# Block attention: reciprocals laid side by side before they are sent, and the tail transpose in a PSUM tile of its own

## The chip, the cores and the metric

The kernel runs on one core of one Trainium2 chip. The metric is device time in microseconds (us), the median of several executions of the whole program; lower is better. One further execution was recorded by the hardware profiler, and every row below comes from it.

## The reference

Three stages in float32. First, attention with a block-causal mask, for 4 batches × 8 heads, 576 positions, 64 features a head; block i of 64 queries sees the keys of blocks 0 to i:

```
scores = q @ k.T / 8;  masked where key block > query block
attn = exp(scores - rowmax) ;  attn /= rowsum + 1e-9
x = attn @ v                       # 2304 tokens x 512 features
```

Then a dense layer pair, `max(0.01 h, h) @ w_out` with `h = x @ w_in` (512 to 2048 and back), and then a mixture of 8 experts (`relu(x @ w1[e]) @ w2[e]`, 512 to 1024 and back) whose weights P come from a softmax of `x @ w_gate`, normalised eight times by rows and columns.

## The kernel before

**Pairs and turns.** Attention works on two heads at once, a pair; there are 16 pairs (`NP`). A loop over p, from -1 to 16, runs one *turn* for each: in turn p the scores of pair p+1 are made (`scores`), the exponentials of pair p are turned by TensorE so that keys lie on partitions (`turn_attn`, seven groups g = 0 to 6), the last products of pair p-1 with v are made (`weigh`), pair p-1 is divided by its softmax sums and split into two parts (`split_x`, L414 to L425), and q and k of pair p+2 are turned (`turn_q`, `turn_k`, `turn_tail`). The order of these steps on TensorE is the list `turns`, written out by hand; TensorE runs exactly in that order. The order on the other engines and on the DMA queues is laid down when the program is built, by a scheduler with its own estimates. Each engine then takes its instructions in that order, and an instruction that waits holds all that stands behind it.

**Blocks, even and odd.** Of the nine blocks of 64 queries the even ones ("straight") keep head 0 on partitions 0 to 63 and head 1 on 64 to 127, and the odd ones ("crossed") the other way round. `ssum` holds the sums of exponentials, one column a block, and a tenth column that block 8 uses for the second half of its keys.

**The way of the sums.** At the start of turn p, `totals(p)` adds 1e-9 on GpSimd (L357), takes reciprocals on VectorE (L358) into `rsum`, 128 partitions × 9 columns, and sends them to DRAM in two transfers (L362): the five even columns to `row0`, the four odd ones to `row1`. `spread_totals(p)`, late in the turn, reads these rows back four times (L371), each broadcast over 64 partitions, into `by_feature`; VectorE uses that in turn p+1 (L414). All of these transfers are issued by the SP queue. On that queue each turn has, in this order as it ran: the two row transfers, four loads of v (L246, L250), the four reads of the rows, six loads of q and k and their tails (L262, L266), now and then one of a weight (L136, L141), and the next turn's row transfers. There is one q, one k and one tails buffer (`qraw`, `kraw`, `tails`).

**PSUM.** TensorE writes into PSUM tiles: four `sc` tiles for scores, two tiles under the tag "tr", taken in turn, for everything that is transposed (pool `ps_tr`), and one `av` tile of two banks for the products with v. A "tr" tile is free again when whatever was transposed into it has been copied out: groups with even g by ScalarE (L390), with odd g by VectorE (L392), q by ScalarE (L278), k by VectorE (L283).

**The tail.** 576 is four times 128 and 64 more. The last 64 rows of q and k of a pair lie in `tails` and are turned together (L309). From pair 2 on the result goes into the first 128 columns of the `av` tile of pair p-2, which at that point of the order is the current pair's and not written yet; ScalarE copies the q half out (L278) and VectorE the k half (L283). Right behind it in `turns` stands `first_product` (L402, L405), which writes other columns of that same `av` tile.

**Weights.** Beside the turns the float64 words of eight weight pieces are changed into float32 pairs, one small step behind each `scores` (L136 to L202). The dense layers and the experts follow on TensorE.

Of the kernel before, what the change touches and what calls it, by code (L numbers as in the profile page):

```python
# [8 lines left out]
F32 = mybir.dt.float32  # L9
# [6 lines left out]
P = 128  # L16
# [20 lines left out]
def block_attention_mlp_moe(  # L37
# [15 lines left out]
    nc = tc.nc  # L53
# [4 lines left out]
    NQ = S // BLK  # L58
# [156 lines left out]
    def attention(att, ps_sc, ps_tr, ps_av):  # L215
# [13 lines left out]
        ex = [att.tile([P, ew], F32, name=f"ex{i}") for i in range(2)]  # L229
        nmax = [att.tile([P, NQ + 1], F32, name=f"nmax{i}") for i in range(2)]  # L230
        ssum = [att.tile([P, NQ + 1], F32, name=f"ssum{i}") for i in range(2)]
        rsum = [att.tile([P, NQ], F32, name=f"rsum{i}") for i in range(2)]
        NPAR = ((NQ + 1) // 2, NQ // 2)
        by_feature = [[att.tile([P, BLK * n], F32, name=f"by_feature{i}{n}") for n in NPAR] for i in range(2)]
        xs = att.tile([P, S], F32, name="xs")
# [40 lines left out]
        def spread(p, src, lo, n):  # L276
            scale = 1.0 / float(D) ** 0.5
            nc.scalar.activation(  # L278
                out=qT[p % 2][:, lo * BLK:(lo + n) * BLK], in_=src[:, 0:n * BLK], func=AF.Copy, scale=scale
            )  # L280

        def place_k(p, src, lo, hi):
            nc.vector.tensor_copy(out=kT[p % 2][:, lo:hi], in_=src)  # L283
# [3 lines left out]
        def av_tile(p):  # L287
            if p not in av:
                av[p] = ps_av.tile([P, 1024], F32, name="av", tag="av")
            return av[p]  # L290
# [11 lines left out]
            place_k(p, km[:, 0:W], 0, W)  # L302

        def turn_tail(p):
            if 0 <= p - 2:
                tail = av_tile(p - 2)
            else:
                tail = ps_tr.tile([P, 512], F32, name="qk_tail", tag="tr")
            nc.tensor.transpose(tail[:, 0:2 * TAIL], tails, ident)  # L309
            spread(p, tail, W // BLK, TAIL // BLK)  # L310
            place_k(p, tail[:, TAIL:2 * TAIL], W, S)
# [41 lines left out]
        rows = {}  # L353

        def totals(p):
            r, s = rsum[p % 2], ssum[p % 2][:, 0:NQ]
            nc.gpsimd.tensor_scalar(out=r, in0=s, scalar1=EPS, scalar2=None, op0=ALU.add)  # L357
            nc.vector.reciprocal(out=r, in_=r)  # L358
            rows[p] = []
            for c, n in enumerate(NPAR):  # L360
                t = dram.tile([2, BLK * n], F32, name=f"row{c}", tag=f"row{c}")
                nc.sync.dma_start(out=t.rearrange("h (q i) -> (h q) i", i=n), in_=r[:, c:NQ:2])  # L362
                rows[p].append(t)

        def spread_totals(p):
# [67 lines left out]
        def first_product(p):  # L433
# [5 lines left out]
            ("nxt", scores, 3, 2), *other_parts[2:], ("prv", split_x), ("nxt", load_v), ("cur", turn_attn, 1),  # L439
            ("nxt", scores, 5, 4), ("cur", turn_attn, 2), ("fol", turn_q),  # L440
            ("nxt", scores, 1, 0), ("fol", turn_tail), ("cur", first_product), ("cur", turn_attn, 3),
            ("nxt", scores, 7, 6), ("fol", turn_k), ("cur", turn_attn, 4),
            ("cur", spread_totals), ("cur", turn_attn, 5), ("cur", turn_attn, 6),
        ]
        opening = [
            ("nxt", scores, 1, 0), ("nxt", scores, 3, 2), ("nxt", scores, 5, 4), ("nxt", scores, 8),
            ("fol", turn_q), ("nxt", scores, 7, 6), ("nxt", load_v), ("fol", turn_k), ("fol", turn_tail),
        ]

# [13 lines left out]
        turn_q(0)  # L463
        turn_k(0)
        turn_tail(0)
        warm(ps_sc, "sc", 3)
        load_qk(1)
# [3 lines left out]
        for p in range(-1, NP + 1):  # L471
            who = {"prv": p - 1, "cur": p, "nxt": p + 1, "fol": p + 2}
            if 0 <= p < NP:
                totals(p)
            if p == NP:
                first_product(p - 1)
            for w, f, *a in (turns if p >= 0 else opening):
                if 0 <= who[w] < NP and (f is not first_product or p < NP - 1):
                    f(who[w], *a)
                if f is scores and p >= 0 and steps:  # L480
                    with ExitStack() as queued:
                        if p + 1 < NP:
                            queued.enter_context(tc.issue_after(getattr(latest[0], "ins", latest[0])))
                        steps.pop(0)()
            if p + 3 < NP:
                load_qk(p + 3)
# [50 lines left out]
    with (  # L537
        tc.tile_pool(name="att", bufs=1) as att,
        tc.tile_pool(name="ps_sc", bufs=4, space=bass.MemoryType.PSUM) as ps_sc,
        tc.tile_pool(name="ps_tr", bufs=2, space=bass.MemoryType.PSUM) as ps_tr,  # L540
        tc.tile_pool(name="ps_av", bufs=1, space=bass.MemoryType.PSUM) as ps_av,
    ):
        with tc.manual_schedule(engines={mybir.EngineType.PE}):
            attention(att, ps_sc, ps_tr, ps_av)
# [677 lines left out]
    for n in range(0, NGR, 2):  # L1222
        p, e, i = groups[n]
# [135 lines left out]
```

## Time and profile before

| | |
|---|---|
| median of 3 runs | 2149.96 us (2146.71 to 2151.47) |
| the profiled execution | 2146.18 us |
| its span, first to last instruction | 2144.4 us |
| TensorE busy, share of the span | 2073.6 us, 97% |
| VectorE, ScalarE, GpSimd busy | 1561.2, 816.5, 654.3 us |
| mean granted TensorE clock | 0.983 of full speed |

The page cuts the span into 40 slices of 53.6 us. In the first six, attention, TensorE is busy 7 or 8 tenths and its clock stands between 0.7 and 0.9 of full speed; from the seventh on it is busy 9 tenths or more at full clock. So the shares of the whole span say little about attention, which has to be read by itself. A turn is measured below from the first score product of block 8 (64x288) to the next one.

### The profile page before, as it was taken

How to read it: one execution, taken by the hardware profiler on the slowest of the kernel's cores; microseconds unless marked ns; L12 is line 12 of the kernel's file. 1: busy time of each engine (PE TensorE's matmuls, PEld its weight loads, DVE VectorE, ACT ScalarE, POOL GpSimd, SP SyncE). 2: the span in 40 equal slices, each digit the busy share in tenths (PEclk: the TensorE clock that was granted, in tenths of full speed). 3: DMA queues.
4: the chain of work that ended last, by engine and by line, in shares of the span. 5: the costliest groups of instructions: out<-in, count | busy, mean ns of one | idle time of the engine just before them, and what ended most of it. 6: DMA issues, size and time to landing. Idle time of an engine off the chain costs nothing.

```text
span 2144.4 us, 32404 instructions
## 1 busy us (share of the span) xinstructions
PE 2073.6 (97%) x11498; PEld 1853.6 (86%) x11498; DVE 1561.2 (73%) x2687; ACT 816.5 (38%) x1795; POOL 654.3 (31%) x639
## 2 busy tenths in 40 slices
PE   8777799999999999999999999999999999999999
PEld 4333368898879888998999999999999999999998
DVE  6554547565644888777878688888888688888886
ACT  5444433222233544544554433223333433333222
POOL 1111213122201354445444133332332223333322
PEclk9897899999999999999999999999999999999999
DMA  5454422011103788888889777777777677777773
GB/s 114 77 86 72 76 43 60 30 60 30 50 10 123 275 320 297 297 307 316 297 297 342 283 276 256 268 254 254 257 270 279 241 259 252 266 263 257 267 257 111
DMA packets 254945, 436.92 MB, mean 204 GB/s; under 512 B 95016, under 2 KB 135976, under 8 KB 254528
## 3 DMA queue, kind: packets, MB, share of 16 engines
q1 hardware_dynamic: 253584, 434.56, 60.8%
q8 instruction: 91, 1.49, 0.3%
q14 instruction: 70, 0.57, 0.1%
q10 hardware_dynamic: 1200, 0.30, 0.1%
HBM read 308.82 MB, written 125.95 MB: 203 GB/s over the span
## 4 chain that ended last, share of the span: by engine, by line
PE 87%; DMA 5%; DVE 4%; ACT 1%; issue 1%; SPq 1%; POOL 0%; DVEq 0%; ACTq 0%; POOLq 0%
PE h_ps L854 28%; PE o L1022 20%; PE o L1078 12%; PE o L533 9%; PE h_ps L513 9%; PE o L854 3%; DMA row<-rsum 2%; PE sc L331 2%; DMA kraw<-in_k_dram 1%; PE tr L383 1%; PE av L405 1%; DMA by_feature<-row 1%; DVE nmax L337 1%; DMA wraw<-in_moe_w_out_dram 1%; DVE xa L951 0%
## 5 line engine op out<-in xcount | busy, mean ns | idle before, releaser
L951 DVE TENSOR_TENSOR xa<-o,xa 128x384 f32<-128x384 f32 x392 | 216.0, 552 | 110.5 <-PE o L1022 106.7
L854 PE MATMUL h_ps<-xhS,w1h 128*128 128x384 f32 x768 | 257.5, 335 | 0.0
L854 PE MATMUL h_ps<-xhS,w1l 128*128 128x384 f32 x768 | 256.6, 334 | 0.0
L854 PE MATMUL h_ps<-xlS,w1h 128*128 128x384 f32 x768 | 256.6, 334 | 0.0
L951 POOL TENSOR_TENSOR xa<-xa 128x384 f32<-128x384 f32 x92 | 106.0, 1152 | 408.1 <-DVE xa L951 370.8
L951 ACT COPY places<-h_ps 128x384 f32<-128x384 f32 x192 | 92.3, 481 | 287.0 <-PE h_ps L854 219.6
L951 ACT CAST xllate<-xa 128x384 fp32r<-128x384 f32 x120 | 61.6, 514 | 279.2 <-POOL xa L951 279.2
L854 PE MATMUL h_ps<-xhA,w1h 128*128 128x384 f32 x448 | 150.8, 337 | 0.1
L854 PE MATMUL h_ps<-xhA,w1l 128*128 128x384 f32 x448 | 150.0, 335 | 0.0
L854 PE MATMUL h_ps<-xlA,w1h 128*128 128x384 f32 x448 | 149.9, 335 | 0.0
L854 PEld LDWEIGHTS h_ps<-xhS,w1h 128*128 128x128 f32 x768 | 144.2, 188 | 0.7 <-issue 0.6
L854 PEld LDWEIGHTS h_ps<-xlS,w1h 128*128 128x128 f32 x768 | 144.2, 188 | 0.0
L854 PEld LDWEIGHTS h_ps<-xhS,w1l 128*128 128x128 f32 x768 | 144.1, 188 | 0.0
L1078 PE MATMUL o<-w2h,xhlate 128*128 128x512 f32 x408 | 143.8, 391 | 0.0
L951 POOL TENSOR_TENSOR places<-places 128x384 f32<-128x384 f32 x60 | 60.9, 1014 | 251.0 <-DVE wa L951 234.0
L1078 PE MATMUL o<-w2h,xllate 128*128 128x512 f32 x384 | 133.9, 389 | 0.0
L1022 PE MATMUL o<-xllate,w2h 128*128 128x384 f32 x480 | 122.4, 335 | 0.0
L1022 PE MATMUL o<-xhlate,w2h 128*128 128x384 f32 x480 | 121.8, 334 | 0.0
L768 POOL TENSOR_TENSOR wa<-wraw 128x256 f32<-128x256 f32 x32 | 29.8, 931 | 296.4 <-DVE w1l L786 279.1
L533 PE MATMUL o<-hh,w2h 128*128 128x512 f32 (+1 forms) x320 | 117.8, 369 | 0.0
L533 PE MATMUL o<-hh,w2l 128*128 128x512 f32 (+1 forms) x320 | 117.7, 368 | 0.0
L521 DVE TENSOR_TENSOR g<-h_ps,g 128x512 f32<-128x512 f32 (+1 forms) x80 | 50.9, 636 | 90.4 <-ACT g L520 90.1
(261 smaller groups left out, 5731.1 us busy)
## 6 DMA issues: line engine op xcount, KB each, us to landing
wraw<-in_moe_w_dram SPq DMA_DIRECT2D x64, 512.0 KB, 4.6
w1h<-k_1h SPq DMA_DIRECT2D x64, 512.0 KB, 5.3
w1l<-k_1l SPq DMA_DIRECT2D x64, 512.0 KB, 6.1
w2h<-k_1h SPq DMA_DIRECT2D x60, 512.0 KB, 6.1
w2l<-k_1l SPq DMA_DIRECT2D x60, 512.0 KB, 6.8
w1h<-k_0h SPq DMA_DIRECT2D x64, 384.0 KB, 3.8
w1l<-k_0l SPq DMA_DIRECT2D x64, 384.0 KB, 4.1
w2h<-k_0h SPq DMA_DIRECT2D x60, 384.0 KB, 4.3
```

Source lines behind the costliest of these rows:

```text
L331: nc.tensor.matmul(sc[o:o + BLK, :], qT[p % 2][r, i * BLK:(i + 1) * BLK], kT[p % 2][r, lo:hi], start=True, stop=True,)
L337: latest[0] = nc.vector.tensor_reduce(out=nm[:, i + s:i + s + 1], in_=sc, axis=AX.X, op=ALU.max, negate=True)
L383: nc.tensor.transpose(tr[:, s].rearrange("p h q -> p (h q)"), ex[p % 2][:, off[i] + c * P:off[i] + (c + 1) * P], swap if i in crossed else ...
L405: nc.tensor.matmul(av[p][r, 512 + P * max(c - 1, 0):512 + S - P], lhsT, a[:, q0:, :], start=c == 0, stop=c == NKC - 1,)
L513: nc.tensor.matmul(ps[:, 0:n], w[:, c, cols], x, start=c == 0 and s == 0, stop=c == KC - 1 and s == 2,)
L521: nc.vector.tensor_tensor(out=g[:, 0:n], in0=ps[:, 0:n], in1=g[:, 0:n], op=ALU.max)
L533: nc.tensor.matmul(ps[:, 0:n], w[:, cut], h[:, 0:n], start=start and m == 0, stop=stop and m == 2)
L768: nc.gpsimd.tensor_tensor(out=one[:, 0], in0=a21, in1=a22, op=ALU.add)
L854: mm = nc.tensor.matmul(ps, w[:, c], x[:, c], start=first and c == 0 and s == 0, stop=c == 1 and s == 2, skip_group_check=True,)
L951: ins = f(*a, **k)
L1022: mm = nc.tensor.matmul(o, a, b, start=i == 0, stop=i == 5)
L1078: mm = nc.tensor.matmul(o, h, w, start=m == 0, stop=m == 11)
```

## The change

Two things. `rsum` becomes 128 × 2 × 5: the sums are read as (even columns, odd columns), so that the five straight reciprocals of a partition lie next to each other and the crossed ones behind them; all ten columns are added to and inverted instead of nine. Each of the two row transfers then reads neighbouring elements of a partition. And `turn_tail` always takes a tile of `ps_tr` (tag "tr") instead of borrowing the `av` tile.

```
-        rsum = [att.tile([P, NQ], F32, name=f"rsum{i}") for i in range(2)]
+        rsum = [att.tile([P, 2, (NQ + 1) // 2], F32, name=f"rsum{i}") for i in range(2)]
...
         def turn_tail(p):
-            if 0 <= p - 2:
-                tail = av_tile(p - 2)
-            else:
-                tail = ps_tr.tile([P, 512], F32, name="qk_tail", tag="tr")
+            tail = ps_tr.tile([P, 512], F32, name="qk_tail", tag="tr")
             nc.tensor.transpose(tail[:, 0:2 * TAIL], tails, ident)
...
         def totals(p):
-            r, s = rsum[p % 2], ssum[p % 2][:, 0:NQ]
+            r, s = rsum[p % 2], ssum[p % 2].rearrange("p (i c) -> p c i", c=2)
             nc.gpsimd.tensor_scalar(out=r, in0=s, scalar1=EPS, scalar2=None, op0=ALU.add)
             nc.vector.reciprocal(out=r, in_=r)
...
-                nc.sync.dma_start(out=t.rearrange("h (q i) -> (h q) i", i=n), in_=r[:, c:NQ:2])
+                nc.sync.dma_start(out=t.rearrange("h (q i) -> (h q) i", i=n), in_=r[:, c, 0:n])
```

## Rows read from the trace of the kernel before

**Rows 1.** Stretches: start:end, length, busy time of each engine, clock, DMA share.

```profile
core 0: us, PE busy (x) PEld busy (x) DVE busy (x) ACT busy (x) POOL busy (x), PEclk, DMA share, GB/s
13.64:26.41 12.77, 10.37 (x82) 5.60 (x82) 7.69 (x20) 7.48 (x27) 0.73 (x3) 1.00 0.36 72
26.41:268.49 242.08, 184.58 (x1275) 91.88 (x1274) 133.26 (x292) 112.00 (x363) 46.05 (x59) 0.86 0.48 80
44.95:62.00 17.05, 13.73 (x99) 6.71 (x98) 10.63 (x24) 8.77 (x28) 1.84 (x3) 0.90 0.54 98
99.22:115.77 16.55, 13.69 (x100) 6.90 (x99) 9.26 (x22) 8.36 (x27) 3.40 (x6) 0.90 0.90 74
209.91:226.41 16.50, 13.18 (x100) 6.65 (x99) 10.12 (x24) 8.87 (x29) 2.16 (x4) 0.93 0.44 96
187.55:209.91 22.36, 15.90 (x100) 8.13 (x99) 10.18 (x23) 8.87 (x29) 5.09 (x6) 0.75 0.37 60
310.00:2144.40 1834.40, 1828.55 (x9823) 1721.43 (x9821) 1391.01 (x2309) 673.48 (x1341) 600.68 (x552) 1.00 0.64 225
```

**Rows 2.** TensorE's waits from 13 to 270 us: total us, times, longest.

```profile
PE av L402 <- DVE kT L283: 25.0, 14, 2.6
PE qm L295 <- DVE at L392: 14.6, 8, 3.3
PE tr L383 <- DVE kT L283: 13.1, 12, 1.5
PE km L301 <- DMA kraw<-in_k_dram: 6.4, 4, 2.6
```

**Rows 3.** VectorE's waits from 26.41 to 268.49 us, same columns.

```profile
DVE xs L414 <- DMA by_feature<-row: 12.1, 8, 3.5
```

**Rows 4.** Waits of the SP queue from 13 to 300 us, same columns.

```profile
SPq L371 <- DMA row<-rsum: 114.6, 21, 8.1
```

**Rows 5.** Timeline of the SP queue, one round: start, length, what is issued.

```profile
86.79 1.26 SPq L362 DMA_DIRECT2D row<-rsum  x2
...
90.05 0.50 SPq L250 DMA_DIRECT2D vraw<-in_v_dram  x1
96.73 2.91 SPq L371 DMA_DIRECT2D by_feature<-row  x4
...
104.44 0.56 SPq L362 DMA_DIRECT2D row<-rsum  x1
```

**Rows 6.** Transfers of the whole kernel: KB each, median us from issue to landing.

```profile
DMA packets 254945, 436.92 MB, mean 204 GB/s; under 512 B 95016, under 2 KB 135976, under 8 KB 254528
...
out_dram<-xa SPq DMA_DIRECT2D x18, 256.0 KB, 2.0
...
kraw<-in_k_dram SPq DMA_DIRECT2D x30, 128.0 KB, 2.9
...
row<-rsum SPq DMA_DIRECT2D x16, 2.5 KB, 10.8
row<-rsum SPq DMA_DIRECT2D x16, 2.0 KB, 11.8
```

**Rows 7.** The instructions that touch rsum, and its transfers' landing times.

```profile
L357 POOL TENSOR_SCALAR rsum<-ssum x16: 242/242/296, 14.1 to 282.8; 128x9 f32<-128x9 f32 x16
...
DMA to landing us min/median/max: 8.9/11.1/12.6
```

**Rows 8.** Timeline around the tail of one turn, all engines.

```profile
106.60 0.33 PE L309 MATMUL av<-ident,tails 128*128 128x128 f32 x1
106.67 0.58 ACT L390 COPY at<-tr 128x512 f32<-128x512 f32 x1
...
107.64 0.60 ACT L278 ACTIVATE qT<-qm 128x512 f32<-128x512 f32 x1
...
108.39 0.23 DVE L283 COPY kT<-av 128x64 f32<-128x64 f32 x1 [1.25 <-ACT qT L278]
...
108.67 0.44 PE L402 MATMUL av<-at,vraw 128*64 128x128 f32 x4 [1.74 <-DVE kT L283]
```

**Rows 9.** Timeline of TensorE in the first turn.

```profile
20.68 0.44 PE L402 MATMUL av<-at,vraw 128*64 128x128 f32 x4 [0.91 <-DVE kT L283]
```

## The prediction

> **What bounds the kernel now.** I read the stretches first. From 310 us on TensorE is busy 1828.6 of 1834.4 us at full clock [rows 1]: nothing in the change touches that part, so whatever attention gives back should come off the end one for one. Attention is another matter. Between the first turn and 268.49 us there are 13 turns in 242.08 us, 18.62 us each, with TensorE busy 76% of the time at a mean clock of 0.86 [rows 1]. Six of these turns are short, 16.46 to 17.05 us, mean 16.70 (the first and last of the six are shown, and one between them); the other seven reach from 18.48 to 22.36 us, and the longest stands in the rows [rows 1]. Short and long mostly alternate, which points to something with a fixed period beside TensorE.
>
> The waits say what it is. TensorE's own list names two kinds [rows 2]. One comes in every turn: the first product with v waits for VectorE's copy of the k tail, 25.0 us in 14 waits. The other comes in the long turns: q's transpose waits for VectorE (14.6 us, 8 times) and k's for its load (6.4 us, 4 times). VectorE was late there because it had itself stood waiting for the rows read back from DRAM, 12.1 us in 8 waits [rows 3]. And these were late because the SP queue stood still: its reads of the rows wait for the rows to land, 114.6 us in all, up to 8.1 us at a time [rows 4].
>
> One round of that queue shows the period. The row transfers are issued at 86.79, the loads of v behind them until 90.55; then the queue holds until 96.73, reads the rows back, issues q and k, and sends the next rows at 104.44 [rows 5]. That is 17.65 us: 9.94 from the rows to their reading, and 7.71 from there to the next rows, nearly all of it issuing. The queue is never ahead; it, and not TensorE, sets the mean length of a turn, and what it makes late is both the spread sums and the next q and k. A row transfer moves 2 or 2.5 KB and takes 10.8 or 11.8 us to land, where 128 KB of k take 2.9 [rows 6]. It never took under 8.9 [rows 7], so it isn't mainly a matter of queueing behind others.
>
> **The change, part by part.**
>
> *The rows.* The two transfers of before read every second element: 128 × 5 and 128 × 4 separate elements, 1152 pieces of 4 bytes. Now each partition's elements are neighbours, so one piece a partition should do: 256 pieces of 20 or 16 bytes. What a landing then takes the trace doesn't show. Below it is bounded by the 2.0 us of the output's store to DRAM, above by today's 8.9 [rows 6, 7]. By proportion 8.9 us over 1152 pieces is 7.7 ns each, 2.0 us for 256, and with 2.0 us of a store's own landing about 4. I take 4; the small size and the piece count put it nearer the store. The round of the queue is then the issue of rows and v, 3.76 us, little or no wait, and 7.71: about 12 us. It stops setting the pace once it is shorter than a turn of TensorE without it, some 15.6 us (below), so any landing below 15.6 − 7.71 = 7.9 us brings the whole gain. After that the rows have slack: sent at the start of a turn, back after some 12 us, wanted 4 us into the next turn.
>
> The gain is what the long turns have over the short ones: 242.08 − 13 × 16.70 = **25 us**. Bounds: 0, if landings stay where they are, to 28, if every turn could be as short as the 16.50 of the last one shown.
>
> *The ten columns.* GpSimd's add takes 242 ns for nine columns [rows 7], and its input now steps by two elements. One column more of ten on an engine busy 46 of 242 us [rows 1] costs nothing; even if it doubled, the rows would leave 0.24 us later, hidden in the slack above. Without that slack it would be 0.24 × 16 = 4 us.
>
> *The tail.* In the turn shown, TensorE makes the tail at 106.60 and the first product at 108.67, 2.07 us later, after waiting 1.74 us for ScalarE to copy q (107.64) and then the tails, and for VectorE (108.39 to 108.62) [rows 8]. In a tile of its own this wait goes. In its place the tail waits for its "tr" tile, last used by group 2, which ScalarE copies out from 106.67 to 107.25 [rows 8]. The latter half of the first product wants that copy anyway. So the tail runs at about 107.4 and the product at 107.6 or 107.7: about 1.05 us earlier. Behind it stands the rest of the turn on TensorE, group 3 and the scores of blocks 7 and 6. Over the 14 waits: **15 us**. Bounds: 25.0, if nothing takes the wait's place, and 0, if another does in full. What is late next: group 3 now waits for the copy of q (ending 108.24), when TensorE is still at the product; k's transpose waits for the two tail copies, done at 108.62, but comes only after group 3 and the scores of blocks 7 and 6; the wait of a later group for k's copy, 13.1 us [rows 2], stays.
>
> *The clock.* Short turns run at a mean clock of 0.90 [rows 1], so a fifth of the time at half speed (1.2 instead of 2.4 GHz), 3.3 us that cost up to 1.65. The first turn, whose wait at this very place was 0.91 us [rows 9], ran at 1.00 throughout, 12.77 us with 82 of the usual 100 products [rows 1]; the long turn with the most waiting stands at 0.75. Waits of 0.7 us instead of 1.74 are nearer to the first turn. All of it back would be 13 × 1.65 = 21 us, none 0; since that turn is one, and has less work in it, I take half, **11 us**. The Trainium skill ("TensorE: Matmul & The Clock Gate", Part 4: PE-mode transpose) says that transposes don't count as work towards the full clock. These turns are full of transposes, and the first turn at 1.00 speaks against the rule mattering here; by it this term would be 0 and the sum 40.
>
> Sum: 25 + 15 + 11 = 51 us. The profiled execution took 2146.18 us, 1.8 more than its span; less 51 that is 2095. The median of the runs is 3.8 us above that execution, and I forecast against it: 2149.96 − 51 = **2099 us**.
>
> **The rivals.**
>
> *VectorE's order becomes the bound.* VectorE is busy 9.3 to 10.6 us of a short turn and ScalarE 8.4 to 8.9 [rows 1]; in a turn of 14.7 us that is up to 72%, in a fixed order, between TensorE's steps. Copies that TensorE waits for (group 1 behind the division, k behind the maxima) may eat what the tail gives. For it: the 13.1 us for k's copy are of this kind already [rows 2]. Against it: the engine is idle for a third of the turn. If the tail's 15 and the clock's 11 go so, the turn stays at 16.70 and only 25 is left: 2125.
>
> *The clock comes back whole* and the tail's wait goes entirely: 25 + 25 + 21 = 71, 2079.
>
> *The landing does not fall.* All pieces of a row go into the same 1.3 KB a head. If it is this that takes 9 us and not their number, the queue's round stays at 17.65, and the tail's 15 us are lost too, since TensorE only arrives earlier at the same wait: no change, 2150. Against it: one transfer of k is 512 pieces of 256 bytes and lands in 2.9 [rows 6]. The Trainium skill ("DMA: Bandwidth & Descriptors", Specifications) gives 512 bytes as the least size for full rate and says that smaller ones are read and rewritten; 20 bytes would still be such a piece, and by that rule alone this rival lives. No row here shows it.
>
> *Slower: the clock falls for good.* Shorter turns hold the same short waits more often. A turn's TensorE work at full clock is 13.7 − 1.65 = 12.05 us, and 1.9 us of waits would be left; at a mean clock c, a share h = 2(1 − c) of the time runs at half, and the turn takes (12.05 + 1.9) / (1 − h/2) = 13.95 / c. It is 18.6, as now, at c = 0.75, the clock of the longest turn shown [rows 1]; at 0.70 it is 19.9, and 13 × 1.3 = 17 us are lost: 2167. Against it: the low clocks stand in the turns with long waits, and these go.
>
> **How the numbers follow.** Both waits go and a part of the clock comes back (40 to 62 us): 0.50. Only the queue's part, up to 40 us: 0.28. Everything, over 62 us: 0.11. The landing stays: 0.06. Slower: 0.05. About 0.2%, 4.3 us, is what a measurement of this kernel can tell from no change. Faster 0.89, same 0.06, slower 0.05. From 2079 (the whole of the second rival) to 2130 (20 us of the queue's 25) the range leaves out the last two cases, and a little of the others: 0.15 to 0.2.
>
> **What would show it.** Right: some 240,600 packets instead of 254,945 (16 × 896 fewer), the rows landing in under 5 us, the SP queue's wait for them below 20 us in all, the waits of q's and k's transposes in the rows gone, all turns near 15 us with a clock of 0.90 or more, and the first product waiting under 0.5 us, with a wait of some 0.7 us ahead of the tail. Wrong: rows still landing at 8 us or more; the turns even but at 16.7, with VectorE's copies at the head of TensorE's waits; a clock at 0.8.

## The result, and the profile after

The changed kernel takes 2086.86 us (median of 4 runs, 2085.88 to 2089.56) against 2148.76 for the kernel before on the same chip: a ratio of 0.9713, 95% interval 0.9696 to 0.9730, so 62 us less. The forecast was 2099, with a range of 2079 to 2130. The profiled execution took 2085.93 us, 60.3 less than the one of before.

The stretches after, from one turn's first score product of block 8 to another's as in [rows 1] (start:end, length, busy time of each engine, clock, DMA share, GB/s):

```profile
core 0: us, PE busy (x) PEld busy (x) DVE busy (x) ACT busy (x) POOL busy (x), PEclk, DMA share, GB/s
13.96:25.60 11.64, 10.33 (x83) 5.60 (x83) 7.68 (x21) 7.46 (x27) 0.73 (x3) 1.00 0.61 128
25.60:208.17 182.57, 157.72 (x1276) 81.99 (x1275) 132.40 (x292) 111.44 (x363) 45.76 (x58) 1.00 0.44 104
95.53:109.86 14.33, 12.14 (x100) 6.31 (x99) 10.98 (x25) 8.76 (x28) 4.08 (x4) 1.00 0.37 87
240.00:2084.00 1844.00, 1838.18 (x9873) 1728.26 (x9871) 1395.91 (x2314) 673.48 (x1342) 599.45 (x552) 1.00 0.63 224
```

Thirteen turns now take 182.57 us, 14.04 each, where they took 242.08 [rows 1]. The difference, 59.5 us, is all but 0.8 of the 60.3. Short and long turns are gone: the thirteen lie between 13.7 and 14.4 us. The clock is 1.00 throughout. TensorE's busy time in these turns fell from 184.58 to 157.72 with the same number of products, because none of them runs at half speed any more.

The transfers of the whole kernel after (KB each, median us to landing):

```profile
DMA packets 240609, 436.92 MB, mean 210 GB/s; under 512 B 80680, under 2 KB 121640, under 8 KB 240192
...
vraw<-in_v_dram SPq DMA_DIRECT2D x32, 128.0 KB, 2.5
...
row<-rsum SPq DMA_DIRECT2D x16, 2.5 KB, 2.4
row<-rsum SPq DMA_DIRECT2D x16, 2.0 KB, 2.9
```

There are 14,336 packets fewer than in [rows 6], exactly the 16 × 896 that were forecast. The rows land in 2.4 and 2.9 us instead of 10.8 and 11.8. The loads of v that stand behind them on the queue land in 2.5; in the kernel before they took 10.2:

```profile
vraw<-in_v_dram SPq DMA_DIRECT2D x32, 128.0 KB, 10.2
```

What the SP queue waits for from 13 to 240 us, against [rows 4] (total us, times, longest):

```profile
SPq L246 <- PE av L402: 40.5, 13, 3.9
...
SPq L368 <- DMA row<-rsum: 2.2, 4, 0.7
```

The wait for the rows has fallen from 114.6 to 2.2 us. The queue is now ahead: its longest wait is for TensorE to be done with a buffer of v.

TensorE's waits in the same stretch, against [rows 2], all those over 2 us:

```profile
PE tr L380 <- DVE kT L283: 17.0, 14, 1.5
PE qk_tail L306 <- ACT at L387: 8.1, 13, 0.6
```

The waits for q, for k and for the tail's copy ahead of the first product are gone. In the last one's place stands the tail's own wait for group 2's copy, 0.62 us a turn. One turn around the tail, against [rows 8]:

```profile
102.97 0.57 ACT L387 COPY at<-tr 128x512 f32<-128x512 f32 x1
...
103.60 0.33 PE L306 MATMUL qk_tail<-ident,tails 128*128 128x128 f32 x1 [0.62 <-ACT at L387]
...
103.86 0.44 PE L399 MATMUL av<-at,vraw 128*64 128x128 f32 x4
```

ScalarE's copy ends at 103.54, the tail starts at 103.60, and the first product follows 0.26 us behind it instead of 2.07.

### The profile page after: what moved, and what is told of

It is laid out like the page before. It is cut to its first block, busy times and chain, and to the rows that moved or that the text cites. A ratio compares the mean times of both kernels' runs of the same rounds, so it can differ in the third digit from the quotient of the medians.

```text
span 2084.1 us, 32404 instructions
## 1 busy us (share of the span) xinstructions
PE 2047.0 (98%) x11498; PEld 1844.2 (88%) x11498; DVE 1562.1 (75%) x2687; ACT 815.7 (39%) x1795; POOL 653.1 (31%) x639
## 4 chain that ended last, share of the span: by engine, by line
PE 93%; DVE 4%; issue 1%; ACT 1%; POOL 0%; DMA 0%; SPq 0%; POOLq 0%; DVEq 0%; ACTq 0%
PE h_ps L851 30%; PE o L1019 21%; PE o L1075 13%; PE o L530 10%; PE h_ps L510 10%; PE o L851 3%; PE sc L328 2%; DVE nmax L334 1%; PE tr L380 1%; PE av L402 1%; ACT ex L341 1%; DVE kT L283 0%; DVE xs L411 0%; ACT at L387 0%; DVE at L389 0%
```

## The experiments

They ran on chips on which the kernel before took 2139 to 2142 us, 7 to 10 less than on the first, while the changed kernel took 2085.95 on one of them and 2086.86 on the first. So ratios to before differ a little by chip, and the variants are set beside each other in us. The edits are shown shortened.

**Each half alone.** The first keeps the change of `rsum` and `totals` and gives `turn_tail` its old branch back; the second is the reverse.

```
# the rows alone                       # the tail alone
-  tail = ps_tr.tile(...)              -  r[:, c, 0:n]   of rsum [P, 2, 5]
+  if 0 <= p - 2: tail = av_tile(p-2)  +  r[:, c:NQ:2]   of rsum [P, 9]
+  else: tail = ps_tr.tile(...)
```

> Only the rows' half of the change: reciprocals side by side, the tail still in the av tile. My theory: the SP queue stops pacing the turns, so all turns become like the six short ones of before, about 16.7 us with a mean clock near 0.90 and the first product still waiting about 1.8 us a turn for the tail's copy (25 us in 14); 25 us are gained, 2124 us. A theory in which the clock was lost by the queue's stalls and not by the tail's wait expects a clock of 0.97 or more and turns of about 15 us: 46 us gained, 2103 us.

Measured: 2118.81 us, ratio 0.9897 (0.9883 to 0.9912), 20 us less than before. The thirteen turns, and TensorE's largest waits in this kernel:

```profile
26.32:240.57 214.25, 173.25 (x1275) 86.99 (x1275) 132.58 (x291) 111.55 (x363) 45.70 (x58) 0.92 0.37 89
```

```profile
PE av L402 <- DVE kT L283: 25.4, 14, 2.6
PE tr L383 <- DVE kT L283: 16.7, 14, 1.5
```

The turns are 16.48 us long, like the short ones of before, with a clock of 0.92 and the first product's 25.4 us of waiting untouched. The first theory holds. That the queue's stalls alone had cost the clock does not.

> Only the tail's half: own PSUM tile, the rows still sent in 4-byte pieces. My theory: the first product's wait goes, but the SP queue's round stays at 17.6 to 18.5 us and TensorE arrives earlier at the same waits for q, k and the division; no more than 6 us are gained, 2143 to 2149 us, and the waits of q's and k's transposes in the trace grow by what the first product saves. If the two halves simply add, 15 us or more (with the clock 35) are gained: 2134 us or less.

Measured: 2138.21 us, ratio 0.9996 (0.9984 to 1.0008). TensorE's waits in it from 13 to 260 us, and the SP queue's from 13 to 285:

```profile
PE qm L295 <- DVE at L389: 22.0, 10, 4.2
...
PE km L301 <- DMA kraw<-in_k_dram: 7.8, 3, 3.4
PE qk_tail L306 <- ACT at L387: 6.3, 11, 0.6
PE qm L295 <- DMA qraw<-in_q_dram: 5.2, 2, 4.2
```

```profile
SPq L368 <- DMA row<-rsum: 101.8, 20, 8.7
```

The first product doesn't wait any more, and the time is the same: q's and k's transposes wait longer than in [rows 2], 35 us in all against 21. Alone the tail's half is worth nothing; behind the rows' half it is worth some 32 us (2118.81 to 2086). The halves don't add.

**Fewer pieces.** In the changed kernel the straight reciprocals are put two columns apart again.

```
-  rsum [P, 2, 5]: one add and one reciprocal over (even, odd) columns
+  t = rsum[p % 2]                       # [P, 20]
+  r = [t[:, 0:NQ:2], t[:, NQ + 1:NQ + 1 + NQ // 2]]
+  ... an add and a reciprocal for each; in_=r[c]
```

> The changed kernel, but the straight reciprocals stand two columns apart again (640 pieces of 4 bytes) and only the crossed ones side by side (128 pieces); two small adds and two reciprocals stand in place of one. My theory, time by the number of pieces: 768 pieces land in 6 to 7 us, the queue's round is 7.7 + 6.5 = 14.2 us, just about the 14.04 us of a turn of the changed kernel, and the time is within 8 us of it: 2087 to 2095 us. If any transfer with separate elements takes some 9 us whatever their number, the round is 16.6 us and 13 turns lose 2.5 us each: 2120 us.

Measured: 2139.12 us, ratio 1.0000 (0.9991 to 1.0009). Its row transfers from 13 to 260 us, and TensorE's largest wait:

```profile
row<-rsum SPq DMA_DIRECT2D x14, 2.5 KB, 9.6
row<-rsum SPq DMA_DIRECT2D x14, 2.0 KB, 2.6
```

```profile
PE qm L295 <- DVE at L393: 30.0, 12, 5.4
```

The straight row by itself lands in 9.6 us, the crossed one, side by side, in 2.6, and the whole gain is gone. So 640 pieces take nearly what 1152 took. My expectation of 6 to 7 us, by proportion, was wrong, and with it the estimate on which the prediction had put the landing. The rival's 2120 us is missed as well: thirteen turns take 229.18 us, 17.6 each, where it had 16.6.

**What makes a piece slow.** One more transfer a turn behind the rows of the changed kernel, to a place in DRAM of its own that nobody reads.

```
+  kind = ("near", "far", "pitch", "fewer")[p % 4]   # for p < 13
+  step = {"near": 1, "far": 128, "pitch": 2, "fewer": 1}[kind]
+  away = dram.tile([64 if kind == "fewer" else P, 5, step], F32, ...)
+  nc.sync.dma_start(out=away[:, :, 0], in_=every second column of rsum)
```

> The changed kernel with one more transfer a turn behind the rows, which nobody reads, in four kinds taken in turn, all of 4-byte pieces: near (640 pieces into 2.5 KB side by side, as the straight row was before), far (640 pieces, each 512 bytes from the next), pitch (640 pieces, every second element of 5 KB) and fewer (320 pieces side by side). If a landing goes by pieces an engine, near, far and pitch take the same 9 us and fewer takes half of it. If it is pieces that fall into the same few hundred bytes of DRAM that wait for one another, far takes 3 to 4 us, pitch about half of near, and fewer as long as near.

Measured: 2106.36 us in one run. The DMA engines' busy tenths in the 12 us from the issue of each kind, 0.3 us a digit, in the order near, far, pitch, fewer:

```profile
DMA  8720641232212320100011102111000090007350
...
DMA  9510639019449469999999953235997513259897
...
DMA  9720452120112321111398521597697378972304
...
DMA  6678797351234641200110100010000000352333
```

Behind *far* the engines are busy again after 3 us. Behind *near* and *fewer*, half as many pieces, they stand nearly still until about 10 us after the issue, and behind *pitch* until about 6. The queue shows the same (start, length of issuing, what; for fewer in an earlier turn):

```profile
61.49 0.56 SPq L366 DMA_DIRECT2D fewer<-rsum  x1
...
67.03 4.87 SPq L374 DMA_DIRECT2D by_feature<-row  x4
...
78.44 0.56 SPq L366 DMA_DIRECT2D near<-rsum  x1
...
81.57 7.69 SPq L374 DMA_DIRECT2D by_feature<-row  x4
...
96.22 0.57 SPq L366 DMA_DIRECT2D far<-rsum  x1
...
99.78 2.83 SPq L374 DMA_DIRECT2D by_feature<-row  x4
```

Four reads that nobody holds back take 2.4 us to issue; behind near they take 7.69 and behind fewer 4.87, ending 10.8 and 10.4 us after the extra transfer, and behind far 6.4 us after it. The completion events in the trace give the landings of all thirteen extra transfers: near 9.7 to 11.3 us after the issue (four of them), fewer 8.9 to 12.9, pitch 5.4 to 7.5, far 3.4 to 4.5 (three each). Pieces that fall close together in DRAM wait for one another; their number matters as far as it falls into the same place. This is the second theory. How close is bounded only roughly: pieces 4 or 8 bytes apart wait, pieces 512 bytes apart hardly do. It also explains the run before: the straight row's 640 pieces fall where they fell before. The Trainium skill ("DMA: Bandwidth & Descriptors", Specifications) says that what is smaller than 512 bytes is read and rewritten. Pieces of one such stretch might have to wait for each other for that reason; these rows agree, but show the waiting and not its cause. Pieces of 20 bytes are also below 512, and 26 instead of 128 of them fall into 512 bytes.

**Is it the wait, or the queue behind the pieces?** The rows in 4-byte pieces, the tail in its own tile, and `spread_totals` called after `load_qk`, so that q and the tails are loaded while the rows land.

```
-            ("cur", spread_totals), ("cur", turn_attn, 5), ("cur", turn_attn, 6),
+            ("cur", turn_attn, 5), ("cur", turn_attn, 6),
...
             if p + 3 < NP:
-                load_qk(p + 3)
+                fetched[0] = load_qk(p + 3)
+            if 0 <= p < NP:
+                spread_totals(p)
```

> The rows in 4-byte pieces as before, the tail in its own tile, and the reading back of the rows is put behind the loads of q and of the tails on the SP queue, instead of ahead of them. My theory, that the queue held by the landing sets the pace: the 2.4 us that those loads take to issue now pass while the rows land, the round falls from 17.65 to about 15.2 us, and the time by 13 x 2.4 to 3 us = 31 to 40 us, to 2110 to 2118 us, though the rows land no sooner. If what counts is how late the rows come back, nothing is gained or a few us are lost: 2143 us or more.

Measured: 2129.86 us (six runs from 2126.88 to 2137.53), ratio 0.9955 (0.9937 to 0.9973): 9 us, between the two. One place on its SP queue:

```profile
109.38 0.51 SPq L250 DMA_DIRECT2D vraw<-in_v_dram  x1
109.98 6.78 SPq L262 DMA_DIRECT2D qraw<-in_q_dram  x2
116.85 1.97 SPq L266 DMA_DIRECT2D tails<-in_q_dram  x1
```

Two loads of q, which need nothing of the rows, take 6.78 us to issue instead of 1.1. The queue's list of waits from 13 to 270 us says what they stand for:

```profile
SPq L266 <- DMA row<-rsum: 25.5, 8, 6.3
SPq L262 <- DMA row<-rsum: 16.6, 3, 5.9
SPq L370 <- DMA row<-rsum: 13.4, 2, 6.9
```

Most of the waiting for the rows now stands ahead of the loads of the tails (L266) and of q (L262), and not ahead of the reading back (L370). The reason is in the program. A landing is counted on a semaphore, and the trace shows eight of these for all transfers, used in turn; a transfer waits until the one that used its semaphore before, nearly always eight transfers earlier, has landed. Behind two rows and four loads of v, here with a load of a weight, that is the second load of q; in most turns it is the first load of a tail. (It is also how the extra transfers above held up the reads behind them.) So the tails' loads stood where the reading back had stood, and only the loads of q, 1.1 us a turn, passed under the landing. Both theories had only the wait for the data in view.

> As the run with the rows read back late (4-byte pieces, own tail tile, reading back behind the loads of q), but the two row transfers are issued by ScalarE's queue instead of SP's. If the loads behind the rows were held because they stand in one queue with the undrained pieces, the loads of q now issue in 1.1 us and land in 3, the round falls to about 15 us and the time by 30 us or more against before. If it is the landing of the rows itself that is waited for, by the reading back and the division, the time stays within 6 us of that run, some 0.5% under before.

Its only edit against the last is `nc.scalar.dma_start` for the two rows. Measured: 2161.77 us, ratio 1.0099 (1.0066 to 1.0131), slower. On ScalarE, one turn:

```profile
69.63 0.52 ACTq L361 DMA_DIRECT2D row<-rsum  x1
70.25 0.27 ACT L389 COPY at<-av 128x128 f32<-128x128 f32 x1 [5.37 <-DMA tails<-in_q_dram]
```

ScalarE stands idle for 5.37 us around the issue, until a load of the tails on the SP queue has landed, whose semaphore the row uses next; the copies that TensorE needs stand behind it. So the time exchanges one wait for another and decides nothing. The trace says more on the question. Around these rows the SP queue issues the reading back of the rows of the pair before, which had landed long before, and VectorE waits for it:

```profile
68.73 2.53 SPq L370 DMA_DIRECT2D by_feature<-row  x4
```

```profile
80.97 1.22 DVE L413 TENSOR_TENSOR xs<-av,by_feature 128x320 f32<-128x320 f32 x2 [7.35 <-DMA by_feature<-row]
```

By the completion events the two reads issued ahead of the first row, at 68.73 and 69.38, land 2.8 and 2.7 us later, and the two behind it, at 70.02 and 70.66, take 10.8 and 10.6. The same is seen in three other turns. So it is not the common queue that holds the loads: pieces sent from ScalarE's queue hold up what the SP queue sends after them.

**The clock.** The rows alone, and TensorE given something to do between the tail and the first product, where it stands still for 1.8 us a turn.

```
+        def fill(p):
+            ps = ps_sc.tile([P, 512], F32, name="warm", tag="sc")
+            for _ in range(10):
+                nc.tensor.matmul(ps[:, 0:P], still, still, start=True, stop=True)
...
-  ("fol", turn_tail), ("cur", first_product)
+  ("fol", turn_tail), ("fol", fill), ("cur", first_product)
# second run: nc.tensor.transpose(ps[:, 0:P], still, ident) instead
```

> Only the rows' half, and TensorE makes ten products of zeros (128x128, into a scores tile, never read) between the tail and the first product, where it otherwise waits 1.8 us a turn for the tail's copy. If it is the standing still at that place that costs the clock, the mean clock of the turns rises from 0.92 to 0.98 or more and the turn falls from 16.5 to about 15.1 us though TensorE does more: 18 us below the run with the rows alone. If the clock has another cause, the time is that of the rows alone or a little above.

> The same with ten transposes of zeros in place of the products. By the rule that transposes don't count as work (the Trainium skill, TensorE: Matmul & The Clock Gate, Part 4) the clock stays at 0.92 and the time at that of the rows alone; if they count, it equals the run with products within 4 us.

Measured: 2110.82 us with products (ratio 0.9865, 0.9850 to 0.9879) and 2104.81 with transposes (0.9838, 0.9822 to 0.9854), against 2118.81 with the rows alone. The thirteen turns, products first:

```profile
28.52:233.48 204.96, 187.91 (x1536) 112.02 (x1535) 132.83 (x292) 111.73 (x363) 45.74 (x58) 1.00 0.38 92
```

```profile
27.57:226.64 199.07, 173.30 (x1405) 95.96 (x1404) 132.84 (x291) 111.56 (x363) 45.74 (x58) 1.00 0.39 95
```

With either filling the clock is 1.00 instead of 0.92, and a kernel with more work for TensorE is faster by 8 and by 14 us. It was the standing still that cost the clock. The ten products, 2.50 us in the trace, are longer than the wait they fill, so their turns take 15.77 us; the transposes, 1.31 us, still leave 0.7 us of waiting and their turns take 15.31. The products' gain is 8 us where I had expected 18, and the two runs differ by 6 us where I had expected 4 at most. That transposes don't count, the rule that the prediction set against its third term, is not what this kernel shows: filled with transposes of zeros, among turns full of transposes, the clock stays whole.

**The order of TensorE.** The first run is the changed kernel again, on the same chip as the other three.

> The changed kernel itself, as it stands, to have it on the same chip as the next three: 2.7 to 3.0% under before.

Measured: 2085.95 us, ratio 0.9748 (0.9727 to 0.9769).

```
# tail behind                                    # k first
-("fol", turn_tail), ("cur", first_product)      -("nxt", scores, 7, 6), ("fol", turn_k)
+("cur", first_product), ("fol", turn_tail)      +("fol", turn_k), ("nxt", scores, 7, 6)
```

> The changed kernel with the tail's transpose put behind the first product in the order of TensorE instead of ahead of it. The first product needs no copy for its first half, so the tail's wait for group 2's copy (8.1 us in 13 waits in the changed kernel) passes under it: 6 to 8 us less than the changed kernel, 0.3 to 0.4%. If the copies of the tail then come too late for k's transpose, nothing is gained and that transpose shows waits.

> The changed kernel with k's transpose put ahead of the scores of blocks 7 and 6. The largest wait left on TensorE, a later group waiting for VectorE's copy of k behind the maxima of these scores (17.0 us in 14 waits), should go, for the copy can run while TensorE makes the scores: 12 to 17 us less than the changed kernel, 0.6 to 0.8%. If VectorE's fixed order puts the copy behind the maxima all the same, the wait stays and the time is the same.

> Both orders together. If the two gains add, 18 to 25 us less than the changed kernel, about 1%; with the tail later and k earlier, k's transpose comes only 0.6 us behind the tail and waits for the tail's copies (done some 1.3 to 2 us after it), so I expect less than the sum: 10 to 15 us.

Measured: tail behind 2081.13 us (ratio 0.9724, 0.9704 to 0.9744), 4.8 below the changed kernel; k first 2072.16 (0.9683, 0.9662 to 0.9703), 13.8 below; both 2076.88 (0.9704, 0.9680 to 0.9729), 9.1 below. Only the second lies in its expected range; the first was to give 6 to 8 and the third 10 to 15. TensorE's largest waits, in the same order:

```profile
PE tr L380 <- DVE kT L283: 16.9, 14, 1.5
PE av L402 <- ACT at L387: 4.3, 14, 1.0
```

```profile
PE qk_tail L306 <- ACT at L387: 8.1, 13, 0.6
PE km L301 <- DVE at L389: 1.6, 2, 0.8
```

```profile
PE km L301 <- DVE at L389: 11.2, 14, 1.1
PE av L402 <- ACT at L387: 4.3, 14, 1.0
```

With the tail behind, its 8.1 us go and half comes back as the second half of the first product waiting for the same copy. With k first the 17.0 us for VectorE's copy of k vanish. Together k's transpose waits 11.2 us for VectorE, by this row for the copy of a group where I had expected the tail's: the two orders are worth less than k first alone, which is the fastest version found.

## Why the prediction was right, and where its sizes were off

*The queue's pace, 25 us.* Right in kind: the rows alone leave turns of 16.48 us, where I had put 16.70. The rows alone gave 20 us in time, on a chip on which the kernel before is itself 10 us faster; the profiles give 242.08 − 214.25 = 27.8 us in the thirteen turns, but across two chips. 25 lies between. The ten columns cost nothing, as argued: GpSimd's add takes 241 ns instead of 242.

*The landing, 4 us.* It was 2.4 and 2.9, and the step to it failed. I had taken the time as going by the number of pieces. 640 pieces took 9.6 us where 1152 in two rows took 10.8 and 11.8, and 640 pieces laid far apart landed in 3.4 to 4.5. What counts is how many fall close together in DRAM. The number came out well by luck, because side by side means fewer pieces there too. In the rival of a landing that does not fall I had named the same place in DRAM as a cause, and drawn the wrong conclusion from it; what I set against it, a load of 256-byte pieces, is not a store of 4-byte ones.

*The queue's round.* I had blamed the instruction that waits for the rows. The loads of v behind the pieces landed late as well (10.2 us), and whatever stood eight transfers behind a row waited for it by the shared semaphore; that is why moving the reading back gave 9 us and not 31 or more.

*The tail, 15 us.* The wait that takes the old one's place was forecast at some 0.7 us, and is 0.62. Between the turns filled with transposes (15.31 us, full clock, the product where it was) and the changed kernel's (14.04) lie 1.27 us, 16.5 in thirteen turns.

*The clock, 11 us.* This is the term that was mis-sized most. I had put the whole of what the short turns lose at up to 21 us and taken half; all of it came back, and the cause was the one argued, the waiting at this place. The whole measures 16.48 − 15.31 = 1.17 us a turn, 15 in thirteen. The one row that spoke for it, the first turn at 1.00, deserved more than half the weight.

So the 59.5 us of the thirteen turns are 27.8 for the queue's pace, 15.2 for the clock and 16.5 for the tail, across three chips; each of the three was forecast a little low, and 51 came out for 62.

*The rivals.* VectorE's copies did not eat the gain: what TensorE waits for the copy of k went from 13.1 to 17.0 us, no more. The clock did not fall. The additive view, that each half brings its part, was not among the rivals, and the prediction's own steps contradict it: as long as the queue paces the turns, TensorE's own savings turn into waiting.

## What to carry to other kernels

Look for the loop with the longest round, which here was a DMA queue; until it is shortened, whatever is saved elsewhere reappears as waiting, and two changes that are worth 20 us and nothing by themselves can be worth over 50 together. A few KB stored in 4-byte pieces side by side in DRAM can hold up for 10 us what is sent after them, on the other queue too: lay the source out so that a partition sends its run in one piece. A transfer that needs nothing of a slow one can still wait for it, through a semaphore that the two share, so read in the trace what it waits for. A wait of 1.8 us in every turn cost TensorE another 1.2 us in clock, so price a short stall at both.

## What the runs showed of the hardware that was not expected

Pieces of 4 bytes wait by place and not by number: with 640 or 320 of them side by side the DMA engines stand nearly idle until some 10 us after the issue, and with 640 of them 512 bytes apart they are busy again after 3. Such a store holds up later transfers that need nothing of it: loads of v behind it on its queue landed in 10.2 us instead of 2.5, and reads on the SP queue behind a store on ScalarE's in 10.6 and 10.8 instead of 2.7 and 2.8. And filling a 1.8 us wait with products or transposes of zeros took the mean clock of the turns from 0.92 to 1.00 and the time down by 8 and 14 us.
